# A diffusion block's kernel on one core: the shift-times-V rows put beside the text scale rows, weight slots exchanged, and the first P copy given to VectorE

## Chip, cores, metric

One NeuronCore of a Trainium2 chip. The metric is the device time of one execution in microseconds (us); lower is better. The profile's span is about 2 us shorter than that time. A run is called slow when it is over 1.5% above the fastest of its kernel.

## The reference

A joint attention block of an image stream (2 x 256 tokens) and a text stream (2 x 32 tokens), D = 1152, all bfloat16:

```python
mod_i = (_silu(c) @ wmod_img).reshape(B, 6, 1, D)      # shift, scale, gate of the image; the same for text
hi = _layernorm(x_img) * (1 + sci) + shi               # ht likewise
qkvi, qkvt = hi @ wqkv_img, ht @ wqkv_txt
q, k, v = ...                                          # text and image tokens joined
p = _softmax(einsum('bqd,bkd->bqk', q, k) * D ** -0.5)
a = einsum('bqk,bkd->bqd', p, v)
out_i = x_img + gai * (a[:, Nt:] @ wo_img)             # out_t likewise
```

## The kernel before

Fourteen weight blocks of 1152 x 1152 (2592 KB each) are streamed through five slots on chip, by loads that SyncE issues strictly in its own order; a load waits until the last reader of its slot is done. The image shift is left out of V and put in later by its product with the V weights. That product is the "shift-times-V rows": 36 small matmuls (32 columns of the array, four side by side), a write of the two result rows to a scratch in DRAM by ScalarE's queue, and four broadcast reads (`svb`) of it by SyncE. Text scale has the same form of rows, without the scratch. These are the parts concerned (`# ...` marks cuts):

```python
    w_sh_i = load_w(2, wmod_img, 0)
    w_q_i = load_rows(3, wqkv_img, 0)
    w_sh_t = load_rows(0, wmod_txt, 0, (0, 1, 3, 6))
    nc.sync.dma_start(x_t[:], xt_flat[:, :])
    w_k_i = load_w(4, wqkv_img, D)
    w_sc_t = load_w(1, wmod_txt, D)
    w_q_t = load_w(2, wqkv_txt, 0)
    # ...
    def mod_rows_of(w, lhs):
        gps = ps_tr.tile([P, KT, LW], f32, tag="tr")
        for kt in range(KT):
            for g in range(NGG):
                mm(gps[LW * g:LW * g + LW], lhsT=lhs[:, kt, :], rhs=group(w, kt, g),
                   start=(kt == 0), stop=(kt == KT - 1), tile_position=(0, LW * g))
        return gps
    # ...
    def qk_img(wq, blk, hooks):
        for j in range(KT):
            for hook in hooks.get(j, ()):
                hook()
            ps = ps_mm.tile([P, B * NI], f32, tag="mm")
            for kt in range(KT):
                mm(ps[:], lhsT=wq[:, kt, j * P:(j + 1) * P], rhs=hT_i[:, kt, :],
                   start=(kt == 0), stop=(kt == KT - 1))
            qk_evac(qkT[:, blk * KT + j, :, 0:NI], ps[:].rearrange("p (b n) -> p b n", b=B), blk)
    # ...
    def shift_v_rows():
        p_sv = mod_rows_of(w_v_i, shT32)
        nc.scalar.copy(svr[:], p_sv[:])
        cols["v"] = mod_cols_of(p_sv, "svc")
        for b in range(B):
            nc.scalar.dma_start(svd[b].rearrange("(c g l) -> g c l", g=NGG, l=LW), svr[b:P:LW])
        for g in range(2):
            for b in range(B):
                r0 = 64 * g + NT * b
                nc.sync.dma_start(svb[r0:r0 + NT, :], svd[b, g * HD:(g + 1) * HD].partition_broadcast(NT))
    # ...
    v_last()
    shift_v_rows()
    w_k_t = load_w(3, wqkv_txt, D)
    w_ga_i = load_w(0, wmod_img, 2 * D)
    w_v_t = load_w(1, wqkv_txt, 2 * D)
    w_o_i = load_rows(4, wo_img, 0)
    w_ga_t = load_w(3, wmod_txt, 2 * D)
    w_o_t = load_rows(1, wo_txt, 0, (0, 5))
    qk_img(w_q_i, 0, {0: (shift_part(0, 2),), 3: (txt_stats, shift_part(2, 4), txt_var, txt_norm),
                      5: (shift_part(4, 7),), 8: (shift_part(7, KT),)})
    qk_img(w_k_i, 1, {1: (txt_transposes,), 4: (txt_rows_scale, shift_blocks, txt_scale),
                      7: (shift_fold, txt_shift), 8: (lambda: qk_txt(0, w_q_t),)})
    qk_txt(1, w_k_t)
    # ...
    # ... scores, softmax, image gate rows, text V ...
    # ...
    pt0, pt1, pt2 = p_transposes(0, ps_tr), p_transposes(1, ps_tr), p_transposes(2, ps_mm)
    v_txt_out(1, vt[1])
    p_out(0, pt0, nc.scalar.copy, 0, 1)
    p_out(0, pt0, nc.vector.tensor_copy, 1, B)
    p_out(1, pt1, nc.scalar.copy, 0, 1)
    p_out(2, pt2, nc.vector.tensor_copy)
    p_out(1, pt1, nc.scalar.copy, 1, B)
    img_gate_spread()
```

## Time and profile before

| | |
|---|---|
| time, median of the runs of this comparison | 117.75 us (117.37 to 118.41, 6 runs) |
| span of the profiled run | 115.7 us, granted clock 1.0 |
| TensorE busy | 95% of the span |
| DMA | about 410 GB/s until 101 us |
| text V weights land / are first used | 80.54 us / 81.94 us |

### The profile page before, as it was taken

The page shows a single profiled execution, that of the slowest core. Times are in us where ns is not written, and L with a number is a line of the kernel's source. Part 1 is how long each engine was busy: PE and PEld are TensorE (multiplying, and loading weights), DVE is VectorE, ACT ScalarE, POOL GpSimd, SP SyncE. Part 2 cuts the span into 40 slices and gives each one's busy share as a digit, 9 for nine tenths or more (in the row PEclk, how much of TensorE's full clock was granted, in tenths as well). Part 3 has the DMA queues.
Part 4 walks back from the last instruction along what each step waited for, and adds up shares of the span by engine and source line. Part 5 has one row for each costly group of instructions (what it writes and reads, how often), then busy time and mean ns, then how long its engine had stood idle before and what let it go on. Part 6 is the DMA issues. An engine that isn't in the chain of part 4 may idle for free.

```text
span 115.7 us, 2570 instructions
## 1 busy us (share of the span) xinstructions
PE 109.6 (95%) x1069; PEld 63.3 (55%) x1078; DVE 72.2 (62%) x152; ACT 43.9 (38%) x93; POOL 12.2 (11%) x32
## 2 busy tenths in 40 slices
PE   4998899999999999999999999999999999999990
PEld 2335644445584444445454458787866566557670
DVE  3469692053868999999996040018768508666671
ACT  4699810042652289825330324244647400100000
POOL 7200000000000000000000000002450700434000
PEclk9999999999999999999999999999999999999998
DMA  3999999999999999999999999999999999942223
GB/s 97 366 378 404 408 406 409 413 410 413 409 403 410 320 387 408 407 410 414 412 363 395 411 404 413 413 409 406 413 404 410 404 421 374 386 167 51 102 51 102
DMA packets 18917, 41.02 MB, mean 355 GB/s; under 512 B 1323, under 2 KB 1851, under 8 KB 18907
## 3 DMA queue, kind: packets, MB, share of 16 engines
q1 hardware_dynamic: 18032, 39.85, 89.7%
q0 software_dynamic: 480, 0.89, 2.2%
q10 hardware_dynamic: 395, 0.12, 0.4%
q8 instruction: 8, 0.13, 0.4%
q14 instruction: 2, 0.02, 0.0%
HBM read 39.52 MB, written 1.34 MB: 353 GB/s over the span
## 4 chain that ended last, share of the span: by engine, by line
PE 84%; ACT 5%; DVE 4%; DMA 3%; issue 1%; DVEq 0%
PE ps L61 52%; PE vps L61 15%; PE gps L61 5%; PE aps L61 5%; PE sps L61 4%; DMA x_i<-in_x_img_dram 3%; ACT xn_i L194 2%; ACT xn_i L195 2%; DVE tmp L721 1%; DVE xT_i L257 1%; PE pT_ps L64 1%; DVE o L722 1%; PE tp L64 1%; PE sc_ps L61 1%; DVE xn_i L209 0%
## 5 line engine op out<-in xcount | busy, mean ns | idle before, releaser
L61 PE MATMUL ps<-xT_i,t 128*128 128x512 bf16 x157 | 35.4, 379 | 0.3
L61 PEld LDWEIGHTS <-t 128*128 128x128 bf16 x333 | 21.0, 98 | 19.1 <-issue 0.7
L450 DVE SCALAR_TENSOR_TENSOR acc_sh<-t,sTf,acc_sh 128x1152 f32<-128x1152 bf16 x16 | 21.4, 1409 | 0.0
L61 PE MATMUL ps<-t,aT 128*128 128x384 bf16 (+3 forms) x153 | 20.3, 308 | 0.0
L61 PE MATMUL vps<-t,hS_i 128*128 128x512 bf16 (+1 forms) x105 | 17.7, 324 | 0.3 <-DVE hS_i L269 0.2
L61 PEld LDWEIGHTS <-aT 128*128 128x128 bf16 (+1 forms) x153 | 13.0, 101 | 7.1 <-issue 0.8
L61 PEld LDWEIGHTS <-hS_i 128*128 128x128 bf16 x108 | 9.0, 98 | 8.9 <-DVE hS_i L269 0.4
L721 DVE TENSOR_TENSOR tmp<-ps,gb 128x384 bf16<-128x384 f32 (+2 forms) x13 | 6.8, 524 | 7.9 <-DMA gb<-mod_scratch 4.0
L380 ACT CAST qkT<-ps 128x512 bf16<-128x512 f32 (+2 forms) x11 | 6.1, 552 | 14.8 <-PE ps L61 13.5
L607 POOL TENSOR_SCALAR pb<-e,rs 128x32 bf16<-128x32 f32 (+1 forms) x5 | 2.3, 459 | 75.9 <-DVE rs L599 75.9
L378 ACT ACTIVATE qkT<-ps 128x512 bf16<-128x512 f32 (+2 forms) x11 | 6.0, 560 | 8.3 <-PE ps L61 6.7
L61 PE MATMUL wps<-warm 128*128 128x512 bf16 x23 | 7.3, 472 | 1.5 <-DVE unit L127 1.5
L177 DVE CAST v_i<-vps 128x512 bf16<-128x512 f32 x5 | 3.5, 692 | 8.0 <-PE vps L61 8.0
L587 DVE TENSOR_REDUCE nmx<-sps 128x1 f32<-128x288 f32 x4 | 1.8, 458 | 9.4 <-PE sps L61 9.4
L179 ACT CAST v_i<-vps 128x512 bf16<-128x512 f32 x4 | 2.3, 581 | 10.1 <-PE vps L61 10.1
L61 PEld LDWEIGHTS <-sT 128*32 128x32 bf16 x180 | 4.5, 96 | 1.8 <-issue 1.2
L61 PE MATMUL sps<-qkT 128*128 128x288 bf16 (+1 forms) x54 | 5.3, 287 | 0.0
L652 DVE TENSOR_SCALAR aT<-aps,svc 128x288 bf16<-128x288 f32 x9 | 4.3, 518 | 1.5 <-PE aps L61 1.5
L61 PE MATMUL gps<-t,sT 128*32 128x288 bf16 x144 | 5.2, 287 | 0.0
L61 PEld LDWEIGHTS <-warm 128*128 128x128 bf16 x25 | 2.6, 112 | 4.9 <-issue 2.1
L61 PE MATMUL aps<-pT,v_i 128*128 128x288 bf16 x36 | 5.1, 287 | 0.0
L61 PE MATMUL ps<-hT_t,t 128*128 128x64 bf16 x162 | 5.1, 193 | 0.0
(112 smaller groups left out, 104.7 us busy)
## 6 DMA issues: line engine op xcount, KB each, us to landing
t<-in_wqkv_txt_dram SPq DMA_DIRECT2D x3, 2592.0 KB, 19.1
t<-in_wmod_img_dram SPq DMA_DIRECT2D x2, 2592.0 KB, 13.8
t<-in_wmod_txt_dram SPq DMA_DIRECT2D x2, 2592.0 KB, 18.4
t<-in_wqkv_img_dram SPq DMA_DIRECT2D x3, 864.0 KB, 13.6
t<-in_wqkv_img_dram SPq DMA_DIRECT2D x1, 2592.0 KB
t<-in_wo_img_dram SPq DMA_DIRECT2D x3, 864.0 KB, 9.9
t<-in_wqkv_img_dram SPq DMA_DIRECT2D x3, 576.0 KB, 10.0
t<-in_wmod_txt_dram SPq DMA_DIRECT2D x2, 864.0 KB, 13.4
```

What stands on the lines that cost most here:

```text
L61: return pin(nc.tensor.matmul(*a, **k))
L64: return pin(nc.tensor.transpose(*a, **k))
L177: nc.vector.tensor_copy(out_ap, in_ap)
L179: nc.scalar.copy(out_ap, in_ap)
L194: pin(nc.scalar.activation(junk, x_ap, ACT.Copy, scale=1.0 / D, accum_out=sm[:, 0:1]))
L195: pin(nc.scalar.activation(junk, x_ap, ACT.Square, scale=float(D) ** -0.5, accum_out=sm[:, 1:2]))
L378: nc.scalar.mul(out_ap, in_ap, SCALE)
L380: nc.scalar.copy(out_ap, in_ap)
L450: pin(nc.vector.scalar_tensor_tensor(acc, w_sh_t[:, kt, :], col, acc, op0=ALU.mult, op1=ALU.add))
L607: pin(nc.gpsimd.tensor_scalar(dst, src, rs[0:qn, :], 0.0, op0=ALU.mult, op1=ALU.add))
L652: nc.vector.tensor_scalar(dst, tiles[(b, dt)][:], bias, None, op0=ALU.add)
L721: nc.vector.tensor_mul(tmp[:, 0:n], ps[:, 0:n], gb[:, b, c0:c0 + n])
```

## The change

Its intent is to pay the switch of TensorE into the 32-column mode and out of it once for two row blocks, not twice, and to let the first P copy start on an engine that is free. As the shift-times-V rows need the image V weights (slot 1), these stay on chip some 24 us longer; so text scale, text q and text k get other slots, and the later loads are issued from inside the k projection. (The keys in the last argument of `qk_img` are column blocks counted from 0; the functions listed under a key run ahead of that block. Key 3 is the fourth block.)

```diff
--- before.py
+++ after.py
@@ -113,8 +113,9 @@
     w_sh_t = load_rows(0, wmod_txt, 0, (0, 1, 3, 6))
     nc.sync.dma_start(x_t[:], xt_flat[:, :])
     w_k_i = load_w(4, wqkv_img, D)
-    w_sc_t = load_w(1, wmod_txt, D)
-    w_q_t = load_w(2, wqkv_txt, 0)
+    w_sc_t = load_w(2, wmod_txt, D)
+    w_q_t = load_w(3, wqkv_txt, 0)
+    w_k_t = load_w(1, wqkv_txt, D)
 
     nc.scalar.preload_act_table_set("natural_log_exp_and_others")
     eps_t = eps_row[:, 0:1]
@@ -562,18 +563,21 @@
                                     gsc[1, b, :].rearrange("(r g j) -> g r j", r=2, g=2)[g].partition_broadcast(NT))
 
     v_last()
-    shift_v_rows()
-    w_k_t = load_w(3, wqkv_txt, D)
-    w_ga_i = load_w(0, wmod_img, 2 * D)
-    w_v_t = load_w(1, wqkv_txt, 2 * D)
-    w_o_i = load_rows(4, wo_img, 0)
-    w_ga_t = load_w(3, wmod_txt, 2 * D)
-    w_o_t = load_rows(1, wo_txt, 0, (0, 5))
+    late = {}
+
+    def late_loads():
+        late["ga_i"] = load_w(0, wmod_img, 2 * D)
+        late["v_t"] = load_w(2, wqkv_txt, 2 * D)
+        late["o_i"] = load_rows(4, wo_img, 0)
+        late["ga_t"] = load_w(3, wmod_txt, 2 * D)
+        late["o_t"] = load_rows(1, wo_txt, 0, (0, 5))
+
     qk_img(w_q_i, 0, {0: (shift_part(0, 2),), 3: (txt_stats, shift_part(2, 4), txt_var, txt_norm),
                       5: (shift_part(4, 7),), 8: (shift_part(7, KT),)})
-    qk_img(w_k_i, 1, {1: (txt_transposes,), 4: (txt_rows_scale, shift_blocks, txt_scale),
+    qk_img(w_k_i, 1, {1: (txt_transposes,), 3: (shift_v_rows, txt_rows_scale, late_loads, shift_blocks, txt_scale),
                       7: (shift_fold, txt_shift), 8: (lambda: qk_txt(0, w_q_t),)})
     qk_txt(1, w_k_t)
+    w_ga_i, w_v_t, w_o_i, w_ga_t, w_o_t = [late[k] for k in ("ga_i", "v_t", "o_i", "ga_t", "o_t")]
 
     aT = act.tile([P, KT, B * NTOK], bf, tag="Q")
     qpos = [[0, P, 2 * P], [NT, NT + P, 0]]
@@ -695,10 +699,10 @@
     v_txt_out(0, vt[0])
     vt.append(v_txt(1))
     pt0, pt1, pt2 = p_transposes(0, ps_tr), p_transposes(1, ps_tr), p_transposes(2, ps_mm)
+    p_out(0, pt0, nc.vector.tensor_copy, 0, 1)
     v_txt_out(1, vt[1])
-    p_out(0, pt0, nc.scalar.copy, 0, 1)
-    p_out(0, pt0, nc.vector.tensor_copy, 1, B)
     p_out(1, pt1, nc.scalar.copy, 0, 1)
+    p_out(0, pt0, nc.scalar.copy, 1, B)
     p_out(2, pt2, nc.vector.tensor_copy)
     p_out(1, pt1, nc.scalar.copy, 1, B)
     img_gate_spread()
```

## The prediction

> **What bounds the kernel now.** I read the page first (busy shares and the 40 slices), then the chain that ended last, then the timeline of SyncE, then single records around the places that the diff touches.
>
> From the page:
>
> ```profile
> PE 109.6 (95%) x1069; PEld 63.3 (55%) x1078; DVE 72.2 (62%) x152; ACT 43.9 (38%) x93; POOL 12.2 (11%) x32
> ...
> PE   4998899999999999999999999999999999999990
> ...
> DMA  3999999999999999999999999999999999942223
> GB/s 97 366 378 404 408 406 409 413 410 413 409 403 410 320 387 408 407 410 414 412 363 395 411 404 413 413 409 406 413 404 410 404 421 374 386 167 51 102 51 102
> ```
>
> Two things are full at once. TensorE has no empty slice from about 12 us to 111 us. The DMA engines run at about 410 GB/s until about 101 us: the fourteen weight blocks (2592 KB each, 6.5 us each at that rate) are simply streamed one after the other. So TensorE sets the end, and the weight stream follows only just ahead of it. The chain says who wins today:
>
> ```profile
> 30.70 2.60 PE vps L61 x38
> 33.31 1.22 PE gps L61 x36
> 34.52 2.05 PE ps L61 x9
> ...
> 57.41 2.75 PE ps L61 x12
> 60.16 1.22 PE gps L61 x36
> 61.38 0.32 PE ps L61
> ...
> 82.22 2.21 PE ps L61 x72
> 84.42 0.94 PE pT_ps L64 x15
> 85.37 5.87 PE aps L61 x54
> ```
>
> It is TensorE without a wait from 14 to 111 us (the 0.05 us "issue" pieces sit where a matmul record is missing). The gps block at 33.31 is the one that moves (shift times V), the one at 60.16 is the text scale rows. SyncE's timeline shows how weight slots gate the stream:
>
> ```profile
> 34.57 3.17 SPq L89 DMA_DIRECT2D t<-in_wmod_txt_dram  x1
> 37.78 7.13 SPq L89 DMA_DIRECT2D t<-in_wqkv_txt_dram  x1
> 45.01 7.65 SPq L409 DMA_DIRECT2D svb<-sv_scratch  x4
> 52.76 0.39 SPq L89 DMA_DIRECT2D t<-in_wqkv_txt_dram  x1
> 58.34 0.39 SPq L89 DMA_DIRECT2D t<-in_wmod_img_dram  x1
> 61.42 3.72 SPq L89 DMA_DIRECT2D t<-in_wqkv_txt_dram  x1
> ```
>
> In order: text scale, text q, the four svb reads, text k, image gate, text V. The issue lengths of 3 to 7 us are back-pressure: the queue is 2 to 3 blocks deep there, so nothing runs dry. The tightest arrival is text V. Its group says
>
> ```profile
> DMA to landing us min/median/max: 19.1/19.1/19.1
> ```
>
> so it lands at 61.42 + 19.1 = 80.5 us, and its first matmul (text V, the 72 "ps" matmuls) starts at 81.9 us: **1.4 us of slack**. The others have more: image gate by about 74 (used 80.8), text gate 76.0 + 17.5 = 93.5 (used 97.0), text output rows 84.9 + 17.0 = 101.9 (used 105.6), text q 61.0 (used 69.2), text k 67.7 (used 73.5).
>
> **What the Trainium skill says.** "TensorEngine Tiling (Array Packing)", Key Properties: changing the tiling mode drains TensorE. The trace agrees: before the 32-column scale rows the weight load idles 0.42 us, after them 0.24 us, and the start-to-start steps of the matmuls there are 309 instead of 216 ns going in and 218 instead of 111 ns coming out.
>
> ```profile
> 60.09 0.98 PEld L61 LDWEIGHTS <-sT 128*32 128x32 bf16 x36 [0.42 <-issue]
> 61.30 0.33 PEld L61 LDWEIGHTS <-t 128*128 128x128 bf16 x3 [0.24 <-issue]
> ```
>
> "DMA: Bandwidth & Descriptors", Queues, rings and completion order: the engines round-robin between queue rows, so a small write on ScalarE's queue should pass SyncE's queued blocks. The trace agrees only in part: the two sv_scratch writes were issued at 35.00 and 35.65, yet the first packet of that queue runs at 39.36 and the last at 41.85, ahead of blocks queued earlier but 4.4 to 6.2 us late. The same page, Rules for kernel authors: a DMA that reads what another wrote must wait for its completion. That is the svb wait on SyncE below.
>
> **The change part by part.**
>
> *Rows merged.* Nothing is added: 36 matmuls leave 33.3 us and are put directly ahead of the 36 scale rows, which themselves move one column block earlier (j = 3, not 4). Saved is one entry and one exit of the 32-column mode: (309 - 216) + (218 - 111) = 93 + 107 = **0.20 us** of TensorE, on the path. The q projection starts 1.3 us earlier, the scale rows 3.3 us earlier (56.8).
>
> *First P copy on VectorE.* Today ScalarE copies the first half and VectorE waits for it:
>
> ```profile
> 84.85 1.00 ACT L639 COPY pT<-pT_ps 128x288 bf16<-128x288 bf16 x3 [1.33 <-PE pT_ps L64]
> ...
> 85.28 0.67 DVE L639 COPY pT<-pT_ps 128x288 bf16<-128x288 bf16 x2 [0.34 <-ACT pT L639]
> ```
>
> The first attention matmul starts 148 ns after the last transpose instead of 56, so at most 0.09 us can be had there. A VectorE copy of that size took 309 ns against 399 on ScalarE (single records). The last v_t subtraction moves behind it, but its reader starts at 86.12, and VectorE ends its new list at about 85.95 as today. Worth **0.05 to 0.1 us**.
>
> *Weight slots.* This is where it can be lost. New order on SyncE: text scale, text q (its slot now opens only when the q projection ends, about 50.9 us), text k (opens when the moved rows end, about 58.15), svb, image gate, text V. Step by step:
> - Text scale's bytes end at 52.5 today, about 51.9 without the scratch writes beside them. Text q issued at 50.9 starts about 1.1 us later (the delay of the first load on an idle queue, 0.73 to 1.77), at 52.0: no hole. It ends at 58.5.
> - Text k, issued 58.15, starts at 59.2, a hole of 0.7 us; ends at 65.7, or 66.2 with 0.5 us for the scratch writes (their 64-byte packets slow the stream around 40 us: slice 14 has 320 GB/s).
> - ScalarE copies the rows at 58.15 to 58.55 and issues the scratch writes at 58.6. With the measured delay of 6.9 us from first issue to last packet they are in at 65.5. Only then can SyncE issue the four svb reads (0.45 us each, to 67.3), and only after them the image gate: first bytes at 68.4, against 66.2 today. A **hole of about 2 us** with nearly nothing queued, since the loads now stand behind svb with no backlog.
> - Text V then lands at 80.54 + 2.2 = 82.75. It is wanted at 81.94 - 0.2 = 81.74: TensorE stalls **1.0 us**. The later blocks arrive 2.2 us later too, but had 3.5 us and over, and gain the 1 us of the stall.
>
> Sum: -0.20 - 0.07 + 1.0 = +0.7 us if the scratch writes take as long as today, -0.3 us if they do not.
>
> **The rivals.**
> 1. *Quick scratch writes.* If the 4.4 us were spent behind the back-pressured issue at 34.57 (it ended at 37.74, and the packets came 1.6 us later), the writes will be quick this time, as text k's issue meets an emptier ring. Then svb goes out at 61 to 63 us, image gate at 64.5, behind text k still in transfer; text V lands near 81.2: no stall, 117.5 us. Against it: the GpSimd-queue writes at 83.99 also came 4.0 us late, with no blocked issue ahead of them.
> 2. *Slow scratch writes.* Late as computed or 1 us more: 118.4 to 119.5 us.
> 3. *ScalarE or VectorE becomes the bound in the k projection.* ScalarE gets 0.4 us of copy and 1.2 us of issue between evacuations that each have about 1.35 us of idle time ahead of them, and six PSUM buffers stand between. VectorE's fold input would be ready at about 62.1, with the fold at 67. I see no stall: 0 us.
> 4. *A late text scale, q or k.* They land about 53, 60 and 67 us; wanted 58, 69 and 73. 0 us.
>
> **Range and chances.** I give 60% to the late scratch writes (stall 0.3 to 2, centre 1.0) and 40% to none worth naming. 117.76 - 0.27 + 0.6 x 1.0 = 118.1 us. The range 117.3 to 119.4 goes from the full gain with no stall to a stall of 1.9 us. Two per cent is 2.36 us: faster would need eight times the gain that I can find, 2%; slower would need a stall of 2.6 us, 5%; within 2%, 93%.
>
> **What would show it.** In the changed profile: one gps block of 72 matmuls near 56.8 us, with one 0.42 and one 0.24 us idle of the weight load; VectorE's P copy no longer waiting for ScalarE; the image gate issued at about 67 (rival 1: 64.5); a drop of the GB/s row around 66 to 68 us; and, in the waits, TensorE waiting for the DMA of the text V weights at about 82 us. If text V lands before 81.7 and the time is still over 117.8, the prediction is wrong in a place that I do not name; if the wait is over 2 us, the scratch round trip was mis-sized.

## The result

The changed kernel took 121.55 us in the median (120.15 to 122.87, 6 runs), against 117.75 us. The ratio is 1.027, 95% interval 1.020 to 1.034: slower, and outside the predicted range. A ratio is the mean time of one kernel's fast runs over that of the other's of the same rounds, so not quite the ratio of the medians; two of the six changed runs, 122.27 and 122.87 us, are slow by the rule above and left out of it. The profiled run (120.6 us, clock 1.0) has a span of 118.4 us, 2.7 us over before.

The page of the changed kernel, rows of the 40 slices (2.96 us each) for TensorE, its granted clock and the DMA rate:

```profile
PE   5968999999999999999999999996499998999990
PEclk9999999999999999999999999999999999999999
...
GB/s 100 375 410 408 403 405 410 416 410 412 409 401 389 314 412 409 411 322 405 408 286 388 284 244 403 410 402 412 404 407 413 412 350 410 412 270 51 125 50 100
```

TensorE now has a hole at 80 to 86 us. The stream has three: at about 52, 60 and 68 us (322, 286, then 284 and 244 GB/s). The list of waits says for what TensorE waited (us in total, times, longest):

```profile
PEld L61 <- DMA t<-in_wqkv_txt_dram: 2.7, 1, 2.7
PE ps L61 <- DMA t<-in_wqkv_txt_dram: 2.4, 1, 2.4
...
PE gps L61 <- DMA t<-in_wmod_txt_dram: 0.4, 1, 0.4
```

The first two are one wait, for text V; the third is a shorter one for the text gate. SyncE's timeline shows where the loads were held up, and SyncE's own waits name the reason:

```profile
50.76 7.71 SPq L89 DMA_DIRECT2D t<-in_wqkv_txt_dram  x2
64.37 2.92 SPq L410 DMA_DIRECT2D svb<-sv_scratch  x4
67.39 0.39 SPq L89 DMA_DIRECT2D t<-in_wmod_img_dram  x1
67.82 0.77 SPq L89 DMA_DIRECT2D t<-in_wqkv_txt_dram  x1
```

```profile
SPq L410 <- DMA sv_scratch<-svr: 6.4, 2, 5.8
```

The image gate leaves at 67.39 us (58.34 before), text V at 67.82 (61.42). The intended parts did happen. In the chain that ended last there is one block of 72 row matmuls where there were two of 36:

```profile
56.84 2.32 PE gps L61 x72
```

By the single records the stretch from the last image V matmul to the image gate rows is 47.53 us instead of 47.75. VectorE's first P copy starts as soon as the transposes are there and no longer behind ScalarE:

```profile
87.16 0.31 DVE L643 COPY pT<-pT_ps 128x288 bf16<-128x288 bf16 x1 [0.77 <-PE pT_ps L64]
```

The first attention matmul follows the last transpose by 63 ns instead of 148. How much of the stream was lost can be read from windows. The columns are the stretch, its length, busy time of TensorE (with its instructions), clock, share of the DMA engines and GB/s. Before:

```profile
50.00:54.00 4.00, 4.00 (x21) 1.00 1.04 412
57.00:62.00 5.00, 4.89 (x53) 1.00 1.05 373
65.00:71.00 6.00, 6.00 (x86) 1.00 1.04 409
```

After:

```profile
50.00:54.00 4.00, 4.00 (x24) 1.00 0.97 341
57.00:62.00 5.00, 4.84 (x85) 1.00 0.97 335
65.00:71.00 6.00, 6.00 (x94) 1.00 0.84 266
```

Against 412 GB/s the three stretches lose 0.5 us before (5 x 39/412, and little else) and 3.75 us after (4 x 71/412 + 5 x 77/412 + 6 x 146/412): 3.2 us more. By the bytes moved, text V's end goes from 79.27 to 82.55 us, 3.3 later.

The clock is the second finding. Of the six runs, the two with a granted clock of 1.0 took 120.15 and 120.6 us. The four with 0.982 to 0.986 took 121.28 to 122.87; the two fast ones among them 121.28 and 121.81.

### The profile page after: what moved, and what is told of

Same layout as the page of the kernel before. It is cut to its first block, busy times and chain, and to the rows that moved or that the text cites. A ratio compares the mean times of both kernels' runs of the same rounds, so it can differ in the third digit from the quotient of the medians.

```text
span 118.4 us, 2568 instructions
## 1 busy us (share of the span) xinstructions
PE 109.0 (92%) x1069; PEld 63.1 (53%) x1078; DVE 72.3 (61%) x152; ACT 43.6 (37%) x93; POOL 12.2 (10%) x32
## 4 chain that ended last, share of the span: by engine, by line
PE 63%; DMA 20%; SPq 5%; ACT 4%; DVE 3%; issue 1%; DVEq 0%
PE ps L61 42%; DMA t<-in_wmod_txt_dram 17%; PE vps L61 15%; SPq L97 5%; PE gps L61 4%; DMA x_i<-in_x_img_dram 3%; ACT xn_i L195 2%; ACT xn_i L196 2%; DVE tmp L725 1%; DVE xT_i L258 1%; DVE o L726 1%; PE tp L64 1%; PE sc_ps L61 1%; DVE xn_i L210 0%; ACT rstd L206 0%
## 5 line engine op out<-in xcount | busy, mean ns | idle before, releaser
L61 PE MATMUL wps<-warm 128*128 128x512 bf16 x23 | 6.8, 451 | 1.5 <-DVE unit L128 1.5
L726 DVE TENSOR_TENSOR o<-tmp,x_i 128x384 bf16<-128x384 bf16 (+2 forms) x13 | 4.5, 343 | 1.2 <-DMA out_dram<-o 0.8
```

Of the source, the lines that this page charges most:

```text
L61: return pin(nc.tensor.matmul(*a, **k))
L726: nc.vector.tensor_add(o[:, c0:c0 + n], tmp[:, 0:n], x_i[:, i, c0:c0 + n])
```

## The experiments

Four theories were on the table. **A**: SyncE stands at the svb reads until the scratch is written, and the loads behind it come late. **B**: the exchanged slots alone starve the stream. **C**: the scratch and svb packets slow it. **D**: the wait for text V makes the clock drop. The kernel before ran beside them: 117.47, 117.56 and 117.41 us. Kernels are compared only within the same rounds. All results were correct. Each intended edit stands as a short diff. After each expectation stand the median, the ratio to the kernel before and its 95% interval; against the mark of 2% only the changed kernel, e5_filler and e6_double_trip are slower, the repeat of the changed kernel is unclear, and the others count as the same.

### P copies alone (e1_pcopy)

```diff
 # the kernel before
+    p_out(0, pt0, nc.vector.tensor_copy, 0, 1)
     v_txt_out(1, vt[1])
-    p_out(0, pt0, nc.scalar.copy, 0, 1)
-    p_out(0, pt0, nc.vector.tensor_copy, 1, B)
     p_out(1, pt1, nc.scalar.copy, 0, 1)
+    p_out(0, pt0, nc.scalar.copy, 1, B)
```

> The kernel before with the new order of the P copies alone. Theory (the loss is in the weight stream) and the rivals agree: this part is worth 0.05 to 0.1 us, so 117.65 us, ratio 0.999. In the trace the first attention matmul should start some 60 ns after the last transpose instead of 148. If it came out slower by 0.5 us or more, the P copies would have a share in the loss.

117.44 us, ratio 0.9997 (0.9982 to 1.0012, 22 runs). In its trace the step from the last transpose to the first attention matmul is 64 ns, as expected. The gain of 0.08 us is real there and too small for the times to show. The P copies have no part in the loss. This trace, whose stream of weights is that of the kernel before, also shows how far such slack varies: text V landed at 81.23 us and was first used at 81.69, 0.46 us of slack and not 1.4.

### svb reads on GpSimd (e2_svb_pool)

```diff
 # the changed kernel
-nc.sync.dma_start(svb[r0:r0 + NT, :], svd[...])
+nc.gpsimd.dma_start(svb[r0:r0 + NT, :], svd[...])
```

> The changed kernel, with the four svb reads issued from GpSimd instead of SyncE. Theory A (SyncE stands at the svb reads until the scratch writes are in, and the loads behind it start late): the image gate goes out at about 58.5 us instead of 67.4, the hole of the stream at 66 to 70 us goes, text V lands near 82.2 us, the stall falls from 2.4 us to 0.5 or less, the text gate is no longer waited for; 117.9 us, ratio 1.001. Rival B (the exchanged slots alone starve the stream): the stall stays above 1.5 us and the time above 119 us.

118.51 us, ratio 1.008 (1.005 to 1.011, 7 runs). The image gate leaves at 58.17 us, the hole at 66 to 70 us is gone, text V lands at 82.64 and TensorE waits 1.2 us for it instead of 2.4. That is most of the loss, and so for A; the expected 117.9 is missed, as the two other holes cost more than I had reckoned.

### svb reads on SyncE, but behind text V (e3_svb_behind)

```diff
 # the changed kernel: the four reads in a function of their own
         late["v_t"] = load_w(2, wqkv_txt, 2 * D)
+        shift_v_reads()
```

> The changed kernel, with the svb reads still on SyncE but behind the image gate and text V loads in its order. Theory A: same as with GpSimd, since only the order of the waits counts: 117.9 us, stall of 0.5 us or less. Rival B: above 119 us. Rival C (it is the scratch and svb packets themselves that slow the stream, wherever they are issued): about as slow as the changed kernel, as they still run before text V has landed.

119.3 us, ratio 1.0145 (1.011 to 1.018, 6 runs). Text V lands at 81.61 us, with only 0.2 us of wait: A holds for the place that it speaks of, and C falls, as the same packets still run. But the time is 1.4 us over the expectation. The wait has moved to the text gate:

```profile
98.43 1.29 PE L61 MATMUL gps<-t,sT 128*32 128x288 bf16 x36 [1.79 <-DMA t<-in_wmod_txt_dram]
```

Its load went out at 81.63 us (79.59 in the changed kernel), when text V had landed; among SyncE's own waits stand 4.2 us for the text V load. The instruction list shows why: with the reads in another place, the load of the text gate waits for the completion counter that text V's load uses. A place in SyncE's order is not free even behind the urgent load.

### The slot exchange alone (e4_slots_only)

```diff
 # the changed kernel with its P copies, rows and reads where they were before
+    shift_v_rows()
     late = {}
...
+    late_loads()
     qk_img(w_q_i, 0, ...
-    3: (shift_v_rows, txt_rows_scale, late_loads, shift_blocks, txt_scale)
+    4: (txt_rows_scale, shift_blocks, txt_scale)
```

> The slot exchange alone: shift-times-V rows, scratch writes and svb reads where they were in the kernel before, scale rows at the fifth column block again, P copies as changed. Only the hole behind text scale is left (text q waits for the q projection, issued at 52.1 us, first bytes 1.9 us later). Theory A: text V about 1.0 us later than before, 0.3 us of slack left, no stall, 117.7 us. Rival B: text V over 2 us late and above 119 us.

118.28 us, ratio 1.006 (1.004 to 1.008, 22 runs). I had expected no loss; there is one, so B has a share. Text q is issued at 52.55 us, and by the bytes the stream loses 2.3 us between 50 and 56.5 us. Text V lands at 82.58 us, 0.3 us late, and the text gate at 97.75. The chain that ended last then runs through the gate's own scratch trip:

```profile
97.79 1.31 PE gps L61 x36
...
99.82 5.50 DMA mod_scratch<-g_sb
```

That trip makes nothing longer: from the gate rows to the end it is 18.67 us, as before. Of the 0.78 us by which this profile's span exceeds that of the kernel before, 0.28 are text V, 0.09 the text gate, and 0.40 lie ahead of the last image V matmul. I can't tie these 0.40 to the exchange; B's share is between 0.4 and the 0.7 us of the times.

### The changed kernel again (after_again)

> The changed kernel unaltered, for a comparison on the chip of this call: about 120.5 us where the granted clock is 1.0, and up to 122.5 us where it is about 0.98. Theory A: two waits of TensorE, of some 2.4 us for text V near 82 us and 0.4 to 1 us for the text gate near 99 us. Theory D (the wait for text V makes the clock drop in some runs): a run with a granted clock of 0.98 shows half clock for some 3 to 4 us soon after the wait.

No edit. 120.94 us, ratio 1.023 (1.019 to 1.028, 6 runs), so a loss of about this size repeats on another call (the interval straddles 2%, so the class is unclear). Its profile fell in a slow run of 125.33 us. Page and timeline of that run:

```profile
PEclk9999999999999999999999999999559999999999
...
86.94 4.51 PE L61 MATMUL ps<-t,hT_t 128*32 128x288 bf16 x72 [5.25 <-DMA t<-in_wqkv_txt_dram]
```

Text V came 2.6 us later than in the first profile, although its load went out at the same time (67.55 us) and the bytes of all engines together were as far (82.5 us): the last of the 16 engines was 4 us behind the mean. From 85.79 us, still within the wait of 5.25 us, the clock records show half clock for 6.83 us, twice what I had expected, and the text V matmuls took 4.51 us instead of 2.39. I use this slow run for the mechanism of the clock only. The profile of e6_double_trip below, which is no slow run, shows the same: a wait of 5.3 us for text V, and half clock for 6.83 us from 86.12. The wait of 2.4 us in the first profile of the changed kernel brought no half clock.

### The wait filled with idle matmuls (e5_filler)

```diff
 # the changed kernel, ahead of text V
+    fps = ps_tr.tile([P, 512], f32, tag="tr", name="fps")
+    for _ in range(12):
+        mm(fps[:], lhsT=warm[:, 0:P], rhs=warm[:], start=True, stop=True)
     vt = [v_txt(0)]
```

> The changed kernel with 12 idle matmuls of 512 columns (2.6 us) ahead of the text V matmuls, in the place of the wait; nothing else moves. Theory D: TensorE is never idle there, so the clock stays at 1.0 in all runs, the time is 120.6 us and the runs over 121 us are gone. If the clock drops come from elsewhere (the first microseconds, the chip), the granted clocks still spread from 0.98 to 1.0 and the times from 120 to 122.5.

120.3 us (120.13 to 120.98, 6 runs), ratio 1.023. The granted clock is 0.996 to 1.0 in all six, and no run exceeds 121 us; beside it the unaltered kernel had runs at 0.972, 0.985 and 0.986 of 121.28 to 125.33 us. D holds as to the clock: with the wait filled it stays up. The wait itself costs some 2.7 us. What the drop adds is less certain, as the waits of runs without a profile are not known. Of the changed kernel's fast runs, those at 0.982 to 0.986 took 121.28 to 121.81 us and those at 0.996 and over 119.83 to 120.6. In the slow profile, 4.8 us longer than the first one, text V starts 2.6 us later, and 2.2 us more are spent between text V and the text gate rows, where the clock is halved. And a long run need not have a low clock: e2_svb_pool had a slow run of 120.76 us and e3_svb_behind one of 121.24, both at 1.0.

### The scratch trip made longer (e6_double_trip)

```diff
 # the changed kernel
+        nc.gpsimd.dma_start(svd2[:, :], svd[:, :])       # one more DRAM to DRAM copy
-nc.sync.dma_start(svb[r0:r0 + NT, :], svd[...])
+nc.sync.dma_start(svb[r0:r0 + NT, :], svd2[...])
```

> The changed kernel with the suspected wait made longer: the scratch rows are copied once more (DRAM to DRAM, on the GpSimd queue) before the svb reads. Theory A: the svb reads on SyncE go out 2 to 4 us later, the image gate and text V behind them just as much, and TensorE's wait for text V grows one for one, to 4.5 to 6.5 us; time about 123 to 125 us, the clock dropping in most runs. Rival B (the slots alone): no change, 120.5 us.

125.8 us, ratio 1.066 (1.061 to 1.070, 6 runs), the clock between 0.959 and 0.972 in every run. The image gate leaves 3.56 us later than in the changed kernel (70.95 against 67.39), text V starts 3.85 us later (88.20 against 84.35): nearly one for one, as A says. TensorE waits for the image gate too here (1.0 us), and the time is 0.8 us over the expectation. This run also gives the term that the prediction needed, because here the stream was empty when the image gate was issued at 70.95 us. Windows of it:

```profile
71.00:72.00 1.00, 1.00 (x13) 1.00 0.29 70
72.00:73.00 1.00, 1.00 (x7) 1.00 0.97 104
73.00:74.00 1.00, 1.00 (x36) 1.00 0.92 341
74.00:75.00 1.00, 1.00 (x40) 1.00 1.03 408
```

The first packet of the block runs at 72.01, 1.06 us after the issue. But the 45 packets of the first microsecond took 345 ns in the mean (91 to 1140) instead of 93, and the rate is full only after 73.5. Counted back from the bytes moved by 74, 75, 76 and 77 us at 412 GB/s, the load behaves as if it had begun at full rate at 72.9 to 73.0 us: **about 2.0 us after its issue**.

### svb on GpSimd, rows one column block earlier (e7_pool_j2)

```diff
 # e2_svb_pool
-    3: (shift_v_rows, txt_rows_scale, late_loads, shift_blocks, txt_scale)
+    2: (shift_v_rows, txt_rows_scale, late_loads, shift_blocks, txt_scale)
```

> The changed kernel with the svb reads on GpSimd and both row blocks one column block earlier (third instead of fourth), so that the slot of text k opens at 56 instead of 58 us. Theory A: the hole of the stream at 59 to 61 us goes too, only that behind text scale stays; text V lands 0.8 us earlier than with the svb reads on GpSimd alone, TensorE waits at most 0.5 us for it, 117.9 us, ratio about 1.003. If the holes do not matter one by one, it stays at 118.5 us.

117.28 us, ratio 0.997 (0.995 to 0.999, 17 runs): better than expected, and ahead of the kernel before. The hole at 60 us is gone, text V lands at 81.68.

### Text q's first third in a tile of its own (e9_split)

```diff
 # e7_pool_j2
-    w_q_t = load_w(3, wqkv_txt, 0)
+    w_q_a = wpool.tile([P, KT, 384], bf, tag="wqa", name="t")        # no slot to wait for
+    w_q_b = wpool.tile([P, KT, D - 384], bf, tag="w3", name="t")
+    nc.sync.dma_start(w_q_a[:], qt_v[:, :, 0:384])
+    nc.sync.dma_start(w_q_b[:], qt_v[:, :, 384:D])
```

> As the kernel with svb on GpSimd and the rows at the third column block, and the first third of text q's columns in a tile of its own (6.9 KB a partition), so that it can be asked for before the q projection ends. Theory A: the hole behind text scale at 52 us goes as well, the stream has none left, text V and the text gate are in time, and only the 0.2 us of the merged rows and 0.06 us of the P copy remain: 117.15 us, ratio 0.996 to 0.998. If the smaller packets (768 and 1536 bytes) slow the stream, it is no better than without the split, 117.3 us or more.

117.03 us (116.74 to 117.69, 22 runs) beside 117.41 us, ratio 0.9975 (0.996 to 0.999). Windows of it:

```profile
50.00:54.00 4.00, 4.00 (x24) 1.00 1.05 388
57.00:62.00 5.00, 5.00 (x31) 1.00 1.06 407
65.00:71.00 6.00, 6.00 (x96) 1.00 1.04 400
```

No hole is left, TensorE waits for no load, and what remains by the times is 0.3 us of gain (0.14 to 0.45 by the interval), the size that the prediction gave the two intended parts. Its one profile doesn't confirm the split: by the records below, text V and gate gain 0.28 us, but the tail loses 0.18. This is the best version found, within 2% of before all the same.

### svb left on SyncE, rows one block earlier (e10_j2_sync)

```diff
 # the changed kernel
-    3: (shift_v_rows, txt_rows_scale, late_loads, shift_blocks, txt_scale)
+    2: (shift_v_rows, txt_rows_scale, late_loads, shift_blocks, txt_scale)
```

> The changed kernel with svb left on SyncE, but both row blocks one column block earlier. Theory A: the whole scratch round trip starts 2 us earlier, so that the image gate goes out at 65.4 us instead of 67.4, reaches the full rate at about 67.4, text V lands near 82.2 and TensorE waits 0.5 to 1.0 us for it: 118.6 us, ratio 1.006 to 1.011. Rival B (slots alone, SyncE's wait does not count): like the kernel with svb on GpSimd and the rows at the third block, 0.997.

117.44 us, ratio 1.000 (0.998 to 1.003, 14 runs). One digit in the place of the rows takes back the whole loss, with SyncE still standing at the reads. The image gate leaves at 64.98 us and text V starts at 82.24 after 0.5 us of wait, both close to the expectation; the time is 1 us better than I had made of them, because the gain of 0.3 us stands against the wait, the text gate is in time, and the clock stays up (0.996 to 1.0 in all runs).

### The split with the rows at the fourth block (e11_split_j3)

```diff
 # e2_svb_pool, with the split of e9_split
```

> The kernel with svb on GpSimd and the rows at the fourth block (1.0079 when it ran), with the split load of text q added. Theory A: of its two holes the one at 52 us goes, worth 0.75 us of the stream; the wait for text V falls from 1.2 us to about 0.4: 117.75 us, ratio 1.001 to 1.003. If the hole at 59 us grows by what the one at 52 us no longer takes (the slot of text k opens no earlier), the gain is less than half of that: ratio 1.005 or more.

118.02 us, ratio 1.004 (1.002 to 1.006, 7 runs), between the two outcomes. The first stretch (50 to 56.5 us) loses 0.33 us instead of 0.49, the second stays at 0.97. Text V is in time, and now the text gate is 0.7 us late. The place of the rows counts for more than the split.

### All side by side

Lost stream is the time between 50 and 72 us that the bytes moved fall short of 412 GB/s. V is the time from the last image V matmul to the first text V matmul, gate that from there to the text gate rows, tail from there to the end, all by single records.

| kernel | lost stream | V | gate | tail | ratio |
|---|---|---|---|---|---|
| before | 0.51 | 48.85 | 15.08 | 18.67 | 1 |
| e1_pcopy | 0.52 | 48.85 | 15.02 | 18.67 | 0.9997 |
| changed | 3.97 | 51.32 | 15.36 | 18.67 | 1.027 |
| e5_filler | 3.57 | 51.54 | 14.95 | 18.66 | 1.023 |
| e6_double_trip | 6.23 | 55.36 | 17.17 | 18.67 | 1.066 |
| e4_slots_only | 2.67 | 49.13 | 15.17 | 18.67 | 1.006 |
| e2_svb_pool | 2.15 | 50.12 | 15.05 | 18.91 | 1.008 |
| e3_svb_behind | 1.57 | 49.07 | 16.78 | 18.66 | 1.0145 |
| e11_split_j3 | 1.86 | 49.08 | 15.68 | 18.84 | 1.004 |
| e10_j2_sync | 1.71 | 49.40 | 15.07 | 18.67 | 1.000 |
| e7_pool_j2 | 1.19 | 49.03 | 15.15 | 18.91 | 0.997 |
| e9_split | 0.58 | 48.63 | 15.02 | 18.85 | 0.9975 |

Lost stream up to some 1.7 us is absorbed by the slack of text V and the gain; above it the loss comes through, at text V or at the text gate, though not in proportion (e4_slots_only loses more stream than e2_svb_pool and is no slower). The exception is e3_svb_behind, with 1.57 us lost and 1.0145: its text gate was held back by SyncE's order, not by the stream. (The slow profile of after_again is left out. The row of e6_double_trip includes half clock in its gate column. The tail is 0.2 us longer where svb is on GpSimd; that was not followed up.)

## Why the prediction was wrong

Right were the **mechanism** and both **gains**. Merged rows: 0.22 us measured, 0.20 predicted. P copy: 85 ns, predicted at most 0.09 us. The image gate was to leave at 67.3 us and left at 67.39, the scratch writes took 6.5 us from first issue to last packet (predicted 6.9), neither ScalarE nor VectorE stalled, and text V was the block that came late. My 60% branch is what happened, but with a stall of 2.4 us, beyond the 0.3 to 2 that I gave it. The prediction's own sign for that, "if the wait is over 2 us, the scratch round trip was mis-sized", points to the wrong term: the round trip was right to 0.1 us, as the image gate's issue shows.

The step that failed is a term of the sum, the **start of a load**: "starts about 1.1 us later (the delay of the first load on an idle queue, 0.73 to 1.77)". That is the delay to the first packet, and it is right as such (1.06 us). What counts for the stream is when the full rate stands as if begun, about 2.0 us (the windows of the doubled trip). The term was used three times. Predicted holes: none, 0.7 us, and about 2; measured losses between 50 and 72 us: 0.70, 1.04 and 2.23, of which 0.51 are in the kernel before too. So the stream ran 3.3 us late, not 2.2. Of the three uses only the last decides in the changed kernel: 67.39 + 2.0 + two blocks of 6.44 us (2592 KB at 412 GB/s) is 82.3 us, against 82.55 by the bytes. What the first two holes lose has been waited out by then, as only some 125 GB/s flow between 67 and 69 us; they bind once the third is gone, as in e2_svb_pool. The kernel before hinted at the right number: its very first load, issued at 0.73, has by 11 us moved what 412 GB/s would have moved since about 2.8 (since 2.3 if counted at 5 us).

Smaller terms failed as well.
- *Landing.* I carried over the distance from the mean end of text V's bytes to its landing, 1.27 us. It was about 1.7 in the changed kernel and 4.4 in one slow run, as the last of 16 engines counts. With the 1.1 us that the stream ran later than predicted this makes the wait 2.4 us in place of 1.0.
- *"The later blocks ... had 3.5 us and over".* The text gate had 3.5 us and lost 6.2 (landing 99.66 against 93.48). 3.3 are the stream's. Of the rest, some falls where the late block meets the gate broadcast on GpSimd's queue, which moved at 93 to 97 us as before, when the text gate had just landed. That is a reading of the rates and not tested by itself. It cost 0.45 us of TensorE by the records.
- *The slack itself.* The 1.4 us of text V and the 3.5 us of the text gate were read from one profile. That of e1_pcopy, with the same stream of weights, has 0.46 us (landed 81.23, used 81.69) and 1.6 us (95.12, 96.70). So up to 1.6 of the 6.2 us that the text gate lost may be no more than this spread.
- *The 64-byte packets.* Slice 14 of the page (320 GB/s) was put down to the scratch writes. In the changed kernel these run at 62.8 to 65 us, where the rate is about 393 GB/s, and slice 14 stands at 314 all the same. The 0.5 us charged to them for text k were not theirs (by these rates it is 0.1); what makes that dip stays open.
- *The clock.* I took a wait to cost its length. The filler run shows that it does so only as long as the clock stays up.

For the profiled run the terms add up: text V starts 2.41 us later than before (81.94 to 84.35, the 0.2 us of the merged rows already in it), the way from there to the text gate rows is 0.29 us longer (0.45 of wait, less the P copy and a little), and the tail is equal: 2.70 us, the difference of the spans. The two fast runs at a lower clock lie 0.7 and 1.2 us higher; how much of that is clock and how much a longer wait is not shown.

Of the rivals, quick scratch writes did not come: first packet 4.3 us after the issue (4.4 before), now with no blocked issue ahead of it. What makes that delay stays open; and so does why the last engine trailed so far in the slow run, and how long the waits were in runs that were not profiled.

## What to carry to other kernels

Where the DMA stream is as full as the bounding engine, list for every load the time from which its slot is free, add the full-rate start (2 us here) and look for the first moment at which nothing is queued; each such hole shifts every later landing. An in-order issuing engine that has to wait for a small round trip should have a backlog of big loads issued ahead of it, or should make the trip earlier: here one column block (2 us) was the difference between 2% and nothing. And price a wait of TensorE with the clock that it may drop (here waits of over 5 us did it, one of 2.4 us did not). Slack read from one profile is one draw: look at a second profile before you spend it.

## What the Trainium skill lacked or had wrong

- "DMA: Bandwidth & Descriptors", Specifications, puts first-byte latency on SyncE's and ScalarE's path at about 0.6 us. Here the first packet came 1.06 us after the issue, and no page has the ramp of such a load: about 2.0 us until it stands as at full rate.
- The same page, Queues, rings and completion order, has the engines alternate between queues by packets. Under a full stream the small writes of ScalarE's queue had their first packet 4.4 us after the issue before the change and 4.3 us after it; the page gives nothing for that.
- "TensorEngine Tiling (Array Packing)", Key Properties, says that a change of mode drains TensorE, and gives no cost. One entry and one exit less were worth 0.22 us.
- "TensorE: Matmul & The Clock Gate", Part 1, has idle windows of 3413 ns bring half clock. The profiles agree and add the length: waits of 5.25 and 5.3 us each brought 6.83 us of half clock, two such windows, and a wait of 2.4 us none. In the slow profile the stretch from text V to the text gate rows took 2.2 us more.
